# Windowed attention with sink keys: 64-row score matmuls on the two halves of the array, two head pairs at a time

## The chip, the cores and the metric

The kernel runs on one core of a Trainium2 chip. The metric is the device time of one execution in microseconds. The core has five engines that run their own instruction streams and wait for each other by semaphores: PE (TensorE, matmuls, with weight loads shown apart as PEld), DVE (VectorE), ACT (ScalarE), POOL (GpSimd) and SP, which here issues the DMA transfers.

## The reference

Three stages follow one another, for 2 sequences of 768 positions.

```python
# 1. attention: 8 heads of 64, each query sees 128 keys back and the first 4 (the sinks)
scores = 1/sqrt(64) * q @ k.T
keep   = (pos_k < n_sink) | ((pos_q - pos_k >= 0) & (pos_q - pos_k < window))   # n_sink 4, window 128
a      = softmax(where(keep, scores, -1e9));  x = a @ v
# 2. MLP, 512 -> 1024 -> 512
h = relu(x @ w_in);  y = (h * sigmoid(conv3(h))) @ w_out
# 3. second attention, 4 experts of width 64, causal, top 2 by a gate
out = sum over chosen e of gate_e * softmax(causal(q_e @ k_e.T / 8)) @ v_e @ wo_e
```

The weights of the MLP come as float64 words and are turned into pairs of float32r numbers (a high and a low part) on the chip.

## The kernel before

Sequences are called b0 and b1. Attention goes over query tiles of 128 positions (`qt`, 6 for each sequence) and, inside a tile, over 4 pairs of heads (`pr`): 24 steps for each sequence. One step is `a1_S` (scores on PE, masked minimum on DVE at L427, exponent on ACT at L430), `a1_T` (PE transposes at L532, copied out by ACT at L494) and `a1_V` (products with the values, L574). Once for each query tile come the row sums' inverse (L489, L490), its transpose (L501) and broadcast through DRAM, the sink keys' part (L554 to L582), the scaling of the output (L516) and its split into high and low parts (L494, L604).

A score tile is [128 queries, up to 260 keys] for one head. A head has only 64 features, and the two heads of a pair lie in partitions 0 to 63 and 64 to 127. The kernel before multiplies with all 128 rows: the query tile of one head is padded with zeros in the other head's 64 rows, so the keys of both heads can stream through. The padded tiles are two buffers of [128, 4 pairs, 2 heads, 128], cleared once at the start (L1151, L1152), and one query tile is loaded by two transfers of 64 partitions (L258). In b0 a head's scores are one matmul of up to 260 columns (L425), in b1 two of 130 (L413), since there each key tile has its own buffer. These are float32 matmuls, and the trace shows two weight loads and two matmul records for each. The value products write 64 output columns for each head (weights 128x64), the two heads of a pair to the two halves of the output partitions.

The order of the work is a table. A phase has stages with a lag in slots; `run_phases` puts step i of a stage into slot `start + floor(lag + i * rate)`, and inside a slot the order of the names in `ORD1` (attention and MLP) or `ORD2` (second attention) decides. Engines work through their streams in that order. The conversion of the MLP weights (L291 to L303 on DVE, L351 on POOL) is cut into pieces that `background` strews over the slots. b1's attention runs in the same slots as the MLP of b0 (L742, L745 to L771, L786). The second attention has scores (L996, L997), transposes (L1034), value products (`a2_V`, L1053, again 128x64 weights) and the output matmul (`a2_W`, L1077), for each query tile in two steps, one for each pair of experts. All PE results go through 8 PSUM buffers called psB.

Of the kernel before, what the change touches and what calls it, by code (L numbers as in the profile page):

```python
# [70 lines left out]
SPLIT_LOAD = (5, 2)  # L71
SPLIT_FROM = (NT, NT)
SPLIT_LO = (1, 1)
LAGS = ((1, 2, 1, 4, 3, 4, 5, 5, 2, 7, 7, 9, 11), (1, 1, 2, 3, 4, 5, 6, 3, 2, 6, 7, 8, 8))
# [3 lines left out]
ORD1 = 's0.hi m.rest a0.more a1.T s1.lo a0.gather m.more m.H a1.gather a1.rB m.gate a0.xl m.Y a1.S a1.sV a1.xl a1.r a0.S a1.halo a0.sL late a0.V a0.rB a0.sV a0.xm a1.more s0.lo a1.sT a0.halo a0.rT s1.hi a1.xm a1.misc a1.V a1.xh a0.sT a0.T a0.misc a1.sL a0.r a1.rT m.conv s1.load s0.load m.misc a0.xh'  # L78
ORD2 = 'q1 c0.V c0.T c0.S0 c1.norm c1.V c1.T c1.S0 out c0.W c0.S1 qlo c0.norm c1.W in c1.S1 q0'
SPLIT_LO_ENG = ('pp', 'pp')  # L80
# [4 lines left out]
ENG_KQ = ('da', 'aa')  # L85
# [4 lines left out]
ATTN_LOADS = ((3, 'q', 0, 2), (3, 'v', 0, 3), (7, 'q', 0, 3), (17, 'v', 0, 4), (11, 'q', 0, 4), (19, 'v', 0, 5), (16, 'q', 0, 5), (21, 'v', 1, 0), (20, 'v', 1, 1), (33, 'v', 1, 2), (35, 'v', 1, 3), (40, 'v', 1, 4), (47, 'v', 1, 5), (19, 'k', 1, 0), (19, 'q', 1, 0), (23, 'k', 1, 1), (24, 'q', 1, 1), (25, 'k', 1, 2), (27, 'q', 1, 2), (30, 'k', 1, 3), (33, 'q', 1, 3), (34, 'k', 1, 4), (37, 'q', 1, 4), (38, 'k', 1, 5), (42, 'q', 1, 5))  # L90
class Kernel:
    def __init__(self, tc, q, k, qd, kd, v, vs, lim, w_in, conv_w, w_out, wqkv, wo, out):
        self.tc, self.nc = tc, tc.nc
        self.q, self.k, self.qd, self.kd, self.v, self.vs, self.lim = q, k, qd, kd, v, vs, lim
# [54 lines left out]
    def consts(self, pool):  # L149
# [10 lines left out]
        self.mEO = [pool.tile([P, 2, KW], F32, name=f"m{i}x") for i in range(3)]  # L160
# [22 lines left out]
    def masks(self):  # L183
# [16 lines left out]
        def rest():  # L200
# [11 lines left out]
            for t in range(2):  # L212
                nc.gpsimd.tensor_copy(self.mEO[2][:, t], self.mEO[0][:, 1 - t])
# [23 lines left out]
    def load_qkv(self, b, n, lo, hi):  # L237
# [7 lines left out]
        if n == "k":  # L245
            hi = min(hi, SPLIT_FROM[b])
            if hi <= lo:
                return
# [136 lines left out]
    def a1_S(self, b, qt, pr):  # L385
# [12 lines left out]
        else:  # L398
            m = self.mEO[2 if self.ring(b, qt) and qt % 2 == 0 else qt % 2]
            N, mask = 2 * KW, m.rearrange("p t c -> p (t c)")  # L400
        split = self.ring(b, qt)
        for j in range(2) if split else ():
            h, me = 2 * pr + j, slice(j * D, (j + 1) * D)
            ts_, cs = slice(0, min(qt + 1, 2)), slice(0 if qt > 1 else 2, KW)
            dst = ps[j][:, :N].rearrange("p (t c) -> p t c", t=ts_.stop)
            nc.tensor.matmul(dst, self.QS[:, h, :], self.KH[:, ts_, h, cs], start=True, stop=False)
            nc.tensor.matmul(dst, self.QS[me, h, :], self.KL[me, ts_, pr, cs], start=False, stop=True)
        for j in range(0 if split else 2):
            if b:
                w = N // min(qt + 1, 2)  # L410
                for c in range(N // w):
                    rhs = t["k", max(qt - 1, 0) + c][:, pr, KW - w :]
                    nc.tensor.matmul(ps[j][:, c * w : (c + 1) * w], t["q", qt][:, pr, j, :], rhs, start=(c == 0),  # L413
                                     stop=(c == N // w - 1), skip_group_check=True)
                continue
            if qt == 0:
                rhs = t["k"][:, 0, pr, 2:]
                dst = ps[j][:, :N]
            elif qt == 1:
                rhs = t["k"][:, 0:2, pr, 2:]  # L420
                dst = ps[j][:, :N].rearrange("p (t c) -> p t c", t=2)
            else:
                rhs = t["k"][:, qt - 1 : qt + 1, pr, :]
                dst = ps[j][:, :N].rearrange("p (t c) -> p t c", t=2)
            nc.tensor.matmul(dst, t["q", qt][:, pr, j, :], rhs, start=True, stop=True)  # L425
# [8 lines left out]

    def ring(self, b, qt):

        return qt >= SPLIT_FROM[b]

    def split_load(self, b, qt, n, hf):

        w = KW if n == "k" else P
        raw = self.wraw[n, b, qt, hf] = self.Wt([P, 4, w], s="raw" + n)
        src = (self.kd if n == "k" else self.qd)[b, :, qt, 4 * hf : 4 * hf + 4, :]
        for r in range(2):
            self.nc.sync.dma_start(raw[r * D : (r + 1) * D], src)

    def split(self, b, qt, n, hf):


        nc = self.nc  # L450
        if not hasattr(self, "QS"):
            self.QS = self.Rt([P, H, P], s="QS")
            ring = self.Kt([P, 2 * H * KW + 2 * NPAIR * KW], F32R, "ring")
            self.KH = ring[:, : 2 * H * KW].rearrange("p (s h c) -> p s h c", s=2, h=H)
            self.KL = ring[:, 2 * H * KW :].rearrange("p (s a c) -> p s a c", s=2, a=NPAIR)
        raw = self.wraw.pop((n, b, qt, hf))
        hs = slice(4 * hf, 4 * hf + 4)
        hi = self.KH[:, qt % 2, hs, :] if n == "k" else self.QS[:, hs, :]
        self.copy(ENG_KQ[b]["kq".index(n)], hi, raw)
        self.wraw["lo", n, b, qt, hf] = raw, hi  # L460

    def split_lo(self, b, qt, n, hf):
        raw, hi = self.wraw.pop(("lo", n, b, qt, hf))
        pr = slice(2 * hf, 2 * hf + 2)
        eng = self.nc.gpsimd if SPLIT_LO_ENG[b]["kq".index(n)] == "p" else self.nc.vector
        for j in range(2):
            rows = slice(j * D, (j + 1) * D) if n == "k" else slice((1 - j) * D, (2 - j) * D)
            r, h = (x.rearrange("p (a j) c -> p a j c", j=2)[rows, :, j, :] for x in (raw, hi))
            lo = self.KL[rows, qt % 2, pr, :] if n == "k" else h
            eng.tensor_tensor(lo, r, h.bitcast(F32), op=ALU.subtract)  # L470

    def split_phase(self, b):

# [5 lines left out]
        def each(fn):  # L479
            return lambda i: fn(*steps[i]) if self.ring(b, steps[i][1]) or steps[i][2] == "k" else None  # L480
# [793 lines left out]
```

## Time and profile before

| | |
|---|---|
| median of 3 runs | 388.13 us (387.78 to 388.64) |
| profiled execution | 388.33 us, of it 386.5 us from the first to the last instruction (the span) |
| PE busy | 97% of the span |
| weight loads busy | 88% |
| DVE busy | 75% |
| ACT, POOL busy | 66%, 38% |
| attention alone / with the MLP of b0 / MLP of b1 / projections and second attention | about 0 to 60 / 60 to 160 / 160 to 245 / 245 to 386 us |

Busy shares are means over stages with different limits, so the prediction reads them by stretches. A matmul's printed duration holds its way through the array; how many follow each other in a given time is read from the chain of waits, which lists the pieces of work that released one another, or from the starts in the timeline. Each record is one pass. A few per cent of the matmul records can be missing.

### The profile page before, as it was taken

Reading aid. Unit: us, or ns where it says so; the run is one execution under the profiler, and the core shown is the slowest. Engines: PE = TensorE matmul, PEld = TensorE weight load, DVE = VectorE, ACT = ScalarE, POOL = GpSimd, SP = SyncE. Lnnn points to the kernel's source line nnn. Section 1 sums busy time; section 2 is a strip of 40 time slices with the busy share of each in tenths; the row PEclk is TensorE's granted clock in tenths of the full one; section 3 lists DMA queues with packets and bytes.
Section 4 is the critical chain, followed back from the end, with each engine's and each line's share of the span. In section 5 each row is a group of like instructions: output and inputs, shape, how many; then the busy total and the mean of one; then the engine's idle time right before and its main releaser. Section 6 shows DMA issues by size and latency. Waiting matters only on the chain.

```text
span 386.5 us, 8883 instructions
## 1 busy us (share of the span) xinstructions
PE 375.2 (97%) x3161; PEld 340.3 (88%) x3161; DVE 289.0 (75%) x849; ACT 256.2 (66%) x743; POOL 146.8 (38%) x248
## 2 busy tenths in 40 slices
PE   7899999979999999999999999999999999999994
PEld 5577778969998999999999999999999899888873
DVE  5689999999999798768865767237779786666711
ACT  4887886654676546545665875439888888778741
POOL 8226323465556264575521322310034325134400
PEclk9999999989999999999999999999999999999999
DMA  6944658333253301010221010000000000010112
GB/s 184 319 132 136 194 171 231 121 111 115 78 164 111 111 2 39 18 30 2 50 55 43 20 43 13 3 2 0 2 2 1 3 27 29 31 56 28 56 48 72
DMA packets 22660, 27.53 MB, mean 71 GB/s; under 512 B 2160, under 2 KB 15824, under 8 KB 22608
## 3 DMA queue, kind: packets, MB, share of 16 engines
q1 hardware_dynamic: 22608, 26.88, 23.0%
q8 instruction: 27, 0.44, 0.5%
q14 instruction: 25, 0.20, 0.2%
HBM read 23.68 MB, written 3.19 MB: 70 GB/s over the span
## 4 chain that ended last, share of the span: by engine, by line
PE 83%; DVE 10%; DMA 3%; issue 2%; ACT 1%; SPq 0%; ACTq 0%; DVEq 0%
PE psB L786 18%; PE psB L742 17%; PE psB L934 9%; PE psB L1053 6%; PE psB L1034 6%; PE psB L1077 5%; PE psB L862 4%; PE psB L413 3%; PE psB L574 3%; PE psB L532 3%; DMA q<-in_q_dram 3%; DVE P L427 3%; PE psB L997 3%; PE psB L996 3%; PE psB L425 2%
## 5 line engine op out<-in xcount | busy, mean ns | idle before, releaser
L786 PE MATMUL psB<-g,wouthf 128*128 128x256 f32 x384 | 70.1, 281 | 0.0
L430 ACT ACTIVATE P<-P,nm 128x260 f32<-128x260 f32 (+2 forms) x96 | 46.6, 487 | 22.4 <-DVE nm L427 22.1
L1022 POOL TENSOR_SCALAR P<-P,r 128x256 f32<-128x256 f32 (+5 forms) x48 | 30.1, 640 | 80.7 <-ACT v L874 29.6
L786 PEld LDWEIGHTS psB<-g,wouthf 128*128 128x128 f32 x384 | 59.2, 189 | 0.0
L742 PE MATMUL psB<-xh,winhf 128*128 128x258 f32 x192 | 57.3, 298 | 1.4 <-ACT PT L494 1.2
L742 PE MATMUL psB<-xh,winlf 128*128 128x258 f32 x192 | 54.9, 286 | 0.0
L742 PE MATMUL psB<-xl,winhf 128*128 128x258 f32 x192 | 54.7, 285 | 0.0
L771 POOL TENSOR_TENSOR g<-ht,g 128x256 fp32r<-128x256 f32 x48 | 34.1, 711 | 53.7 <-ACT g L765 49.6
L786 PE MATMUL psB<-g,woutlf 128*128 128x256 f32 x192 | 54.0, 281 | 0.0
L758 ACT ACTIVATE ht<-ht 128x256 f32<-128x256 f32 x48 | 20.1, 418 | 33.4 <-DVE ht L756 33.3
L742 PEld LDWEIGHTS psB<-xh,winhf 128*128 128x128 f32 x192 | 36.9, 192 | 2.2 <-ACT PT L494 1.4
L763 DVE SCALAR_TENSOR_TENSOR ht<-ht 128x256 f32<-128x256 f32 x48 | 23.6, 491 | 19.0 <-ACT ht L758 19.0
L742 PEld LDWEIGHTS psB<-xl,winhf 128*128 128x128 f32 x192 | 37.1, 193 | 0.0
L742 PEld LDWEIGHTS psB<-xh,winlf 128*128 128x128 f32 x192 | 36.9, 192 | 0.0
L786 PEld LDWEIGHTS psB<-g,woutlf 128*128 128x128 f32 x192 | 36.3, 189 | 0.0
L765 ACT CAST g<-ht 128x256 fp32r<-128x256 f32 x48 | 19.1, 398 | 18.5 <-DVE ht L763 17.4
L1007 ACT ACTIVATE P<-P,nm 128x256 f32<-128x256 f32 (+3 forms) x48 | 26.7, 558 | 6.2 <-DVE nm L1001 5.7
L756 DVE SCALAR_TENSOR_TENSOR ht<-ht,cw 128x256 f32<-128x256 f32 x48 | 28.8, 601 | 1.7
L532 PE MATMUL psB<-ident,P 128*128 128x128 f32 x176 | 29.7, 286 | 0.1
L574 PE MATMUL psB<-PT,v 128*64 128x128 f32 x352 | 29.7, 286 | 0.0
L749 POOL TENSOR_SCALAR ht<-ht,cw 128x256 f32<-128x256 f32 x24 | 16.6, 690 | 32.1 <-ACT ht L745 27.2
L1001 DVE CUSTOM_DVE_ANT_0 P<-psB,causal 128x256 f32<-128x256 f32 (+3 forms) x48 | 22.6, 487 | 6.8 <-PE psB L997 6.5
(168 smaller groups left out, 1043.0 us busy)
## 6 DMA issues: line engine op xcount, KB each, us to landing
raw<-in_w_in_dram SPq DMA_DIRECT2D x8, 512.0 KB, 3.4
raw<-in_w_out_dram SPq DMA_DIRECT2D x8, 512.0 KB, 3.7
q<-in_q_dram SPq DMA_DIRECT2D x24, 128.0 KB, 4.4
v<-in_v_dram SPq DMA_DIRECT2D x12, 256.0 KB, 3.6
R<-rD SPq DMA_DIRECT2D x24, 128.0 KB, 3.1
out_dram<-ot SPq DMA_DIRECT2D x11, 256.0 KB, 2.0
k<-in_k_dram SPq DMA_DIRECT2D x8, 260.0 KB, 4.0
raw<-in_wqkv_dram SPq DMA_DIRECT2D x8, 193.0 KB, 2.5
```

What stands on the lines that cost most here:

```text
L430: nc.scalar.activation(Pt[:, j, :N], Pt[:, j, :N], AF.Exp, bias=nmx[:, j : j + 1], scale=-1.0, accum_out=sums[:, j : j + 1])
L532: nc.tensor.transpose(ps[:, j, c, :], Pt[:, j, c0 : c0 + P], self.ident)
L574: nc.tensor.matmul(o[j * D : (j + 1) * D, pr, :], t["v", kt][:, h * D : (h + 1) * D], PT[:, j, c, :], start=(pr == 0 and c == 0), stop=(qt ...
L742: nc.tensor.matmul(ps[:, :XW], w[:, f, kc, :], x[:, kc, :], start=(i == 0), stop=(i == len(ops) - 1))
L756: nc.vector.scalar_tensor_tensor(t1, h[:, 2 : 2 + CH], self.cw[:, 2 * NF + f : 2 * NF + f + 1], t1, op0=ALU.mult, op1=ALU.add)
L763: nc.vector.scalar_tensor_tensor(t1, t1, 1.0, h[:, 1 : 1 + CH], op0=ALU.add, op1=ALU.mult)
L771: eng.tensor_tensor(g[:, 1], t1, g[:, 0].bitcast(F32), op=ALU.subtract)
L786: nc.tensor.matmul(self.m1y[d // 2][:, d % 2, :], w[:, f, d, :], g[:, k], start=(first and i == 0 and d % 2 == 0), stop=(last and i == 2), ...
L934: nc.tensor.matmul(ps, w[:, kc, c0 : c0 + P], y[:, kc, :], start=(i == 0), stop=(i == len(ops) - 1))
L1007: nc.scalar.activation(Pt[:, lo:hi], src, AF.Exp, bias=nm[:, 0:1], scale=sg, accum_out=sums[:, j, i : i + 1])
L1022: nc.gpsimd.tensor_scalar(Ps[j][:, :N], Ps[j][:, :N], r[:, j : j + 1], 1.0, op0=ALU.mult, op1=ALU.mult)
L1034: nc.tensor.transpose(ps[:, s, :], Ps[j][:, c * P : (c + 1) * P], self.ident)
```

## The change

The query buffers hold no zeros any more: there are four of [128, 4 pairs, 128] in the same memory, and a query tile is one transfer of 128 partitions with 2 KB for each partition in one piece. A score matmul takes 64 rows of queries and 64 rows of keys, and goes over one key tile (up to 130 columns) in both sequences. The two heads of a pair alternate, so that neighbouring matmuls use the upper and the lower rows of the array. A stage can have a group size g: step i is then put where the first step of its group stands. Scores and value products of the first attention, and value products and output matmul of the second, have g = 2. The lag of b1's value products goes from 3 to 4 slots, the names in `ORD1` stand in another order (a1.V and a0.V right behind a1.S and a0.S), and one value tile of b1 is loaded 3 slots earlier. Code for a split of the scores that no step used (`ring`, `split_*`), and a third mask with its two copies on POOL, are gone.

```diff
-        for m, (lag, fn) in enumerate(stages):
+        for m, (lag, fn, *g) in enumerate(stages):
             for i in range(n):
-                at.setdefault(o + math.floor(lag + i * rate), []).append((k, m, i, fn))
+                first = i - i % g[0] if g else i
+                at.setdefault(o + math.floor(lag + first * rate), []).append((k, m, i, fn))
...
-LAGS = ((1, 2, 1, 4, 3, 4, 5, 5, 2, 7, 7, 9, 11), (1, 1, 2, 3, 4, 5, 6, 3, 2, 6, 7, 8, 8))
+LAGS = ((1, 2, 1, 4, 3, 4, 5, 5, 2, 7, 7, 9, 11), (1, 1, 2, 4, 4, 5, 6, 3, 2, 6, 7, 8, 8))
...
-                t[n, tt] = self.qbuf[tt % 2]
-                for j in range(2):
-                    rows = slice(j * D, (j + 1) * D)
-                    self.nc.sync.dma_start(t[n, tt][rows, :, j, :], src[rows, tt].rearrange("p (a c) -> p a c", c=P))
+                t[n, tt] = self.qbuf[(b * NT + tt) % len(self.qbuf)]
+                self.nc.sync.dma_start(t[n, tt], src[:, tt].rearrange("p (a c) -> p a c", c=P))
...
+        w = N // min(qt + 1, 2)
+        for c in range(N // w):
+            for j in range(2):
+                rows = slice(j * D, (j + 1) * D)
+                kt = t["k", max(qt - 1, 0) + c] if b else t["k"][:, max(qt - 1, 0) + c]
+                nc.tensor.matmul(ps[j][:, c * w : (c + 1) * w], t["q", qt][rows, pr, :], kt[rows, pr, KW - w :],
+                                 start=(c == 0), stop=(c == N // w - 1), skip_group_check=True)
...
-            "xm": (xm, last(self.x_norm)), "S": (0, each(self.a1_S)), "T": (tr, each(self.a1_T)),
-            "V": (pv, each(self.a1_V)), "gather": (gather, each(self.a1_gather)), "sT": (sT, last(self.a1_sinkT, 2)),
+            "xm": (xm, last(self.x_norm)), "S": (0, each(self.a1_S), 2), "T": (tr, each(self.a1_T)),
+            "V": (pv, each(self.a1_V), 2), "gather": (gather, each(self.a1_gather)), "sT": (sT, last(self.a1_sinkT, 2)),
...
-              "V": (A2_V, each(self.a2_V)), "W": (A2_V + 1, each(self.a2_W))}
+              "V": (A2_V, each(self.a2_V), 2), "W": (A2_V + 1, each(self.a2_W), 2)}
...
-                self.qbuf = [self.Rt([P, NPAIR, 2, P], F32, "q") for _ in range(2)]
+                self.qbuf = [q[:, i] for q in (self.Rt([P, 2, NPAIR, P], F32, "q") for _ in range(2)) for i in range(2)]
```

How the order moves is shown at three places. The first is PE in the middle of b0's attention, before: two steps. L425 are scores (one row a head), L574 value products (two heads in each row), L532 four transposes; the names are PSUM buffer, then the operands.

```order
L425 MATMUL psB_404<-k_124,q_117 128x260
L425 MATMUL psB_405<-k_124,q_117 128x260
L574 MATMUL psB_351<-PT_335,v_131 64x128 x2
L574 MATMUL psB_351<-PT_335,v_133 64x128 x2
L532 MATMUL psB_419<-ident,P_373 128x128 x4
L425 MATMUL psB_434<-k_124,q_117 128x260
L425 MATMUL psB_435<-k_124,q_117 128x260
L574 MATMUL psB_351<-PT_364,v_131 64x128 x2
L574 MATMUL psB_351<-PT_364,v_133 64x128 x2
L532 MATMUL psB_448<-ident,P_406 128x128 x4
```

The same place after the change (scores are L397 there, value products L495, transposes L453); two more score rows of the first pair of heads stand ahead of these.

```order
L397 MATMUL psB_405<-k_119,q_117 128x130
L397 MATMUL psB_406<-k_119,q_117 128x130
L397 MATMUL psB_417<-k_119,q_117 128x130
L397 MATMUL psB_418<-k_119,q_117 128x130
L397 MATMUL psB_417<-k_119,q_117 128x130
L397 MATMUL psB_418<-k_119,q_117 128x130
L495 MATMUL psB_362<-PT_333,v_124 64x128 x2
L495 MATMUL psB_362<-PT_333,v_126 64x128 x2
L495 MATMUL psB_362<-PT_379,v_124 64x128 x2
L495 MATMUL psB_362<-PT_379,v_126 64x128 x2
L453 MATMUL psB_438<-ident,P_352 128x128 x4
L453 MATMUL psB_453<-ident,P_407 128x128 x4
```

Scores of two steps, value products of two steps and transposes of two steps now stand together, and the scores run straight into the value products.

The second place is PE near the end of the second attention, before: value products of the last two query tiles (L1053) and the output matmul (L1077) of the tile ahead of each; zh and zl are the two parts of the attention's result.

```order
L1053 MATMUL psB_5469<-PT_1062_5355,v_710_3968 64x128 x4
L1077 MATMUL psB_5474<-wohf,zh_5446 128x512 x2
L1077 MATMUL psB_5474<-wolf,zh_5446 128x512 x2
L1077 MATMUL psB_5474<-wohf,zl_5447 128x512 x2
L1053 MATMUL psB_5469<-PT_1069_5393,v_710_3968 64x128 x4
L1053 MATMUL psB_5492<-PT_1072_5410,v_710_3968 64x128 x4
L1053 MATMUL psB_5492<-PT_1074_5417,v_723_4034 64x128 x4
L1053 MATMUL psB_5492<-PT_1076_5424,v_736_4098 64x128 x2
```

After the change (value products L972, output matmul L996):

```order
L972 MATMUL psB_5500<-PT_1066_5401,v_710_3989 64x128 x4
L972 MATMUL psB_5500<-PT_1069_5415,v_710_3989 64x128 x4
L996 MATMUL psB_5513<-wohf,zh_5509 128x512 x2
L996 MATMUL psB_5513<-wolf,zh_5509 128x512 x2
L996 MATMUL psB_5513<-wohf,zl_5510 128x512 x2
L972 MATMUL psB_5523<-PT_1076_5452,v_710_3989 64x128 x4
L972 MATMUL psB_5523<-PT_1078_5459,v_723_4055 64x128 x4
L972 MATMUL psB_5523<-PT_1080_5466,v_736_4119 64x128 x2
```

Both value products of the last tile but one (psB_5500) are now neighbours, and the output matmul that reads their result (zh_5509) is the very next instruction; before, the first products of the last tile stood between.

The third place is SP at the start, before: transfers in the order in which they are issued (k, q and v tiles of b0, the raw weights, the row sums rD).

```order
L251 DMA k_124<-in_k_dram 128x1040
L258 DMA q_117<-in_q_dram 64x4x128 x2
L261 DMA v_238<-in_v_dram 128x512
L505 DMA rD_284<-rT_282 8x128
L265 DMA vs_315<-in_vs_dram 128x512
L258 DMA q_118<-in_q_dram 64x4x128 x2
```

After the change:

```order
L243 DMA k_119<-in_k_dram 128x1040
L248 DMA q_117<-in_q_dram 128x512
L251 DMA v_228<-in_v_dram 128x512
L426 DMA rD_278<-rT_276 8x128
L255 DMA vs_325<-in_vs_dram 128x512
L248 DMA q_117<-in_q_dram 128x512
```

The order is the same; each query tile is one transfer, and the third and fourth tile go to the second buffer (two slots of q_117) and no longer overwrite tiles that are still read.

## Rows read from the trace of the kernel before

**Rows 1.** The page's chain that ended last: share of the span by engine

```profile
PE 83%; DVE 10%; DMA 3%; issue 2%; ACT 1%; SPq 0%; ACTq 0%; DVEq 0%
```

**Rows 2.** Stretches: length, busy PE, PEld, DVE, ACT, POOL, then clock, DMA share, GB/s

```profile
24.00:53.00 29.00, 28.77 (x229) 21.14 (x230) 28.40 (x89) 24.82 (x79) 13.34 (x29) 1.00 0.57 170
53.00:98.00 45.00, 42.83 (x373) 38.09 (x370) 43.93 (x118) 27.41 (x90) 22.05 (x35) 0.96 0.50 146
98.00:120.00 22.00, 22.00 (x199) 20.78 (x198) 21.52 (x51) 14.44 (x43) 11.70 (x20) 1.00 0.33 104
120.00:160.00 40.00, 39.78 (x356) 37.54 (x355) 35.23 (x90) 24.76 (x74) 19.45 (x37) 1.00 0.20 60
```

**Rows 3.** Chain of waits around 28 us, b0: start us, us, what

```profile
27.50 0.60 DVE xl L604
28.10 0.34 DVE P L427
...
28.80 0.60 DVE f64u L303
```

**Rows 4.** Chain of waits, then timeline of DVE, at the third query tile

```profile
9.95 8.72 DMA q<-in_q_dram
...
19.52 0.43 DVE L427 CUSTOM_DVE_ANT_0 P<-psB,m0x 128x260 f32<-128x260 f32 x1 [1.78 <-PE psB L425]
```

**Rows 5.** Chain of waits, a step of b0 and scores of a b1 step

```profile
43.01 0.88 PE psB L425 x4
43.89 0.59 PE psB L574 x8
44.47 0.59 PE psB L532 x4
...
123.72 0.89 PE psB L413 x8
```

**Rows 6.** Groups by form: weight loads of scores and value products; last numbers busy, mean ns

```profile
L413 PEld LDWEIGHTS psB<-k,q 128*128 128x128 f32 x176 | 21.6, 191 | 0.0
L574 PEld LDWEIGHTS psB<-PT,v 128*64 128x64 f32 x352 | 18.2, 136 | 10.1 <-issue 5.4 <-ACT xh L494 0.7 <-DVE xl L604 0.3
```

**Rows 7.** Timeline of PEld, value products at 41.65 us: start us, us, what

```profile
41.65 0.14 PEld L574 LDWEIGHTS psB<-PT,v 128*64 128x64 f32 x2 [0.34 <-issue]
```

**Rows 8.** Chain of waits in the second attention

```profile
290.82 1.09 PE psB L1034 x10
...
354.74 0.37 PE psB L1053 x4
...
366.76 1.02 PE psB L1053 x16
367.79 1.24 PE psB L1034 x10
...
376.57 1.59 PE psB L1077 x6
```

**Rows 9.** Instructions of L413 alone in a stretch: length, busy PE, PEld

```profile
120.00:160.00 40.00, 7.39 (x56) 6.84 (x56) 1.00 0.20 60
```

**Rows 10.** Group of the copy that the output matmul waits for

```profile
L132 ACT CAST zh<-psB 128x256 fp32r<-128x256 f32 x11 | 4.0, 366 | 1.6 <-PE psB L1053 1.4
```

**Rows 11.** Timeline of SP at the start: start us, us, what

```profile
1.64 1.37 SPq L258 DMA_DIRECT2D q<-in_q_dram  x2
...
3.70 1.26 SPq L258 DMA_DIRECT2D q<-in_q_dram  x2
5.00 1.08 SPq L261 DMA_DIRECT2D v<-in_v_dram  x2
```

**Rows 12.** A stretch at the start, columns as in rows 2

```profile
12.00:18.00 6.00, 5.59 (x38) 3.69 (x36) 4.58 (x21) 5.32 (x21) 0.00 (x0) 1.00 1.06 338
```

**Rows 13.** A stretch at the lower clock (columns as in rows 2)

```profile
80.00:82.00 2.00, 0.79 (x4) 0.78 (x4) 1.97 (x5) 1.18 (x3) 1.08 (x2) 0.79 0.06 20
82.00:84.00 2.00, 2.00 (x12) 2.00 (x11) 2.00 (x8) 1.51 (x5) 2.00 (x4) 0.50 0.87 280
```

**Rows 14.** Chain of waits: the same MLP matmuls at the lower and the full clock

```profile
81.23 2.95 PE psB L742 x12
...
86.99 1.43 PE psB L742 x12
```

More of the change, by code (lines that the diff above doesn't have):

```diff
@@ L77 @@
 EVT = 'aaadadada'
-ORD1 = 's0.hi m.rest a0.more a1.T s1.lo a0.gather m.more m.H a1.gather a1.rB m.gate a0.xl m.Y a1.S a1.sV a1.xl a1.r a0.S a1.halo a0.sL late a0.V a0.rB a0.sV a0.xm a1.more s0.lo a1.sT a0.halo a0.rT s1.hi a1.xm a1.misc a1.V a1.xh a0.sT a0.T a0.misc a1.sL a0.r a1.rT m.conv s1.load s0.load m.misc a0.xh'
+ORD1 = 'm.rest a0.more a1.T a0.gather m.more m.H a1.gather a1.rB m.gate a0.xl m.Y a1.S a1.V a1.sV a1.xl a1.r a0.S a0.V a1.halo a0.sL late a0.rB a0.sV a0.xm a1.more a1.sT a0.halo a0.rT a1.xm a1.misc a1.xh a0.sT a0.T a0.misc a1.sL a0.r a1.rT m.conv m.misc a0.xh'
 ORD2 = 'q1 c0.V c0.T c0.S0 c1.norm c1.V c1.T c1.S0 out c0.W c0.S1 qlo c0.norm c1.W in c1.S1 q0'
-SPLIT_LO_ENG = ('pp', 'pp')
 ENG_G = 'pp'
@@ L159, in consts @@
         self.m1 = pool.tile([P, 2 * P], F32, name="m1")
-        self.mEO = [pool.tile([P, 2, KW], F32, name=f"m{i}x") for i in range(3)]
+        self.mEO = [pool.tile([P, 2, KW], F32, name=f"m{i}x") for i in range(2)]
     def limits(self):
@@ L211, in rest @@
                 pen(e, m[:, 1, 0:2], snk[:, 2 - first : 4 - first])
-            for t in range(2):
-                nc.gpsimd.tensor_copy(self.mEO[2][:, t], self.mEO[0][:, 1 - t])
         self.more_masks = rest
@@ L398, in a1_S @@
         else:
-            m = self.mEO[2 if self.ring(b, qt) and qt % 2 == 0 else qt % 2]
+            m = self.mEO[qt % 2]
             N, mask = 2 * KW, m.rearrange("p t c -> p (t c)")
[L401 to L425, printed above, removed]
+        w = N // min(qt + 1, 2)
[5 more added lines that the diff above has]
+                                 start=(c == 0), stop=(c == N // w - 1), skip_group_check=True)
         for j in range(2):
@@ L433, in a1_S @@
         self.a1Pg[(b, qt, pr)] = Pt
[L435 to L472, printed above, removed]
-        f = max(SPLIT_FROM[b] - 1, 0)
-        steps = [(b, qt, n, hf) for qt in range(f, NT) for hf in range(2) for n in "kq"]
-        rate = RATE1 if b else 1
-        at = (4 * f - 3) * rate
-        def each(fn):
-            return lambda i: fn(*steps[i]) if self.ring(b, steps[i][1]) or steps[i][2] == "k" else None
-        st = {"load": (at - SPLIT_LOAD[b], each(self.split_load)), "hi": (at, each(self.split)),
-              "lo": (at + SPLIT_LO[b], each(self.split_lo))}
-        n = len(steps) if SPLIT_FROM[b] < NT else 0
-        return lambda names: (b * NSTEP, n, [st[n] for n in names.split()], rate)
     def a1_r(self, b, qt):
@@ L526, in a1_T @@
         else:
-            cols = [KW + 2, 2] if self.ring(b, qt) and qt % 2 == 0 else [2, KW + 2]
+            cols = [2, KW + 2]
         nb = len(cols)
@@ L650, in go0 @@
                 if i == at:
[L651 to L652 removed]
+                    self.load_qkv(bb, n, lo, lo + 1)
             if i >= 4:
@@ L1198, in program @@
                 a0, a1 = first
-                src = {"a0": a0, "a1": a1, "m": m, "s0": self.split_phase(0), "s1": self.split_phase(1), "late": late}
+                src = {"a0": a0, "a1": a1, "m": m, "late": late}
                 ph = self.order(ORD1, src)
@@ L1210 @@
     lim = lim.bitcast(I32)[None, :].to_broadcast([P, 4])
-    K = Kernel(tc, q, k, qd, kd, v, vs, lim, w_in, conv_w, w_out, wqkv, wo, out)
+    K = Kernel(tc, q, k, v, vs, lim, w_in, conv_w, w_out, wqkv, wo, out)
     with tc.tile_pool(name="const", bufs=1) as cpool:
```

23 lines of the change are left out of this document (5 added, 18 removed).

## The prediction

> **What bounds the kernel now.** I read the chain that ended last first: 83% of the span is PE, 10% DVE, 3% a transfer [rows 1]. That is a mean, so next the stretches [rows 2]. From 24 to 120 us DVE has 93.85 of 96 us busy, and the chain runs through it, item behind item, softmax next to weight conversion [rows 3]; PE looks as busy there, but where DVE fills its time a shorter matmul only makes PE wait. From 120 to 160 us PE is full and DVE idles 4.77 us: here a shorter matmul counts until DVE is full too. From 160 us on nearly all of the chain is PE, with no attention score of the changed kind in it; the second attention at its end is changed in its value products. At the start the chain holds one transfer, 8.72 us from the issue of the third query tile to its landing [rows 4], and DVE idles 1.78 us behind it.
>
> So the reader has to keep two sums: what PE is spared, and how much of it DVE lets through.
>
> **The scores on PE.** A step of b0 takes 0.88 us for four records of 260 columns, a step of b1 0.89 us for eight of 130 [rows 5], so 0.22 and 0.111 us a record; PE streams them one behind the other. After the change every step has eight records of 130 columns and 64 rows (half as many of 128 columns in each sequence's first tile). Nothing in this trace uses half the rows. The nearest thing uses half the columns: the value products. There two weight loads with a mean of 136 ns [rows 6] are done within 0.14 us [rows 7], so both halves load at once, and 4 records take 0.37 us, 16 take 1.02 [rows 8]: (1.02 - 0.37) / 12 = 0.054 us a record, and 0.37 - 4 x 0.054 = 0.15 fixed. One record alone needs about 0.11, as the scores of b1 show, so two run side by side.
>
> For the new scores the ends are these. If halves of rows work as halves of columns do, two steps (16 records) cost 1.02 us, the 0.15 included. If they don't, they cost 16 x 0.111 + 0.15 = 1.93, slightly more than now (1.77). I take 1.02: it is the row that also packs two matmuls into the array.
>
> The Trainium skill has a rule against this: by its page "TensorE: Matmul & The Clock Gate", section "LDWEIGHTS (loading the stationary operand)", a weight load takes its time by columns, and one of 32 rows takes as long as one of 128. No load here has fewer than 128 rows, so no row shows it. By it each score load stays at the 191 ns of [rows 6], hidden behind matmuls of the other half only if both halves may load at once; if not, the sum is that of the first rival below. The Trainium skill says on the same page, section "Part 3: Packing small matmuls", that loads overlap running matmuls of another row group, which speaks for 1.02.
>
> **Changing between shapes.** Transposes right behind value products take 1.24 us for ten, elsewhere 1.09 [rows 8]: 0.15 us on leaving the half-array shape, and about 0.15 on entering it (the fixed part above). Before, a step has two such changes, a pair of steps four. After, a pair has three: full to scores, scores to value products, back to full. The Trainium skill, "TensorEngine Tiling (Array Packing)", section "Key Properties", says that a change of the tiling mode drains the array; the trace agrees with its 0.15 us. Counted by it the scores, which used to be free of this, now pay too, and that is in the sum here.
>
> **A pair of steps on PE.** Before: 2 x (0.88 + 0.59 + 0.59) = 4.12 us for scores, value products and transposes [rows 5]. After: 1.02 + 1.02 + 0.15 + 8 x 0.109 = 3.06 (0.109 being a tenth of 1.09). Spared: 1.06 us a pair, 0.53 a step. Over 20 pairs, and some 0.6 in each of the 4 shorter ones, PE is spared 23 us. If all of that counted, the kernel would gain 6%; it won't.
>
> **What counts of it.**
>
> 24 to 120 us: DVE's work is not changed (two clears at the start are gone, before the first scores), and its idle time is 0.60 + 1.07 + 0.48 = 2.15 us [rows 2]. No more than that can be won, and nothing is the other end. I take 1.1. What is late next here is DVE itself.
>
> 120 to 160 us: 56 records of L413 [rows 9] are 7 steps, 7 x 0.53 = 3.7 us spared on PE; DVE has 4.77 us to spare. The two don't wait at the same moments, and four score buffers are now asked for at once instead of two. Ends 0.5 and 3.7, I take 2.8.
>
> Second attention: in the PE order 23 groups of value products become 12. Each one less saves 0.15 + 0.15: 11 x 0.30 = 3.3 us, and PE is the chain there [rows 8]. Against it stands one new wait. The output matmul of the last tile but one now stands directly behind its value products, and needs ACT's copy of them, 0.37 us [rows 10]; before, value products of the last tile covered that (the 1.59 us in [rows 8] for its six records hold no such wait). Behind it on PE stand the last 20 value products, so the end waits. Price 0.37 to 0.73 (the copy twice over, for the hand-overs). Net 2.6 to 2.9; I take 2.6.
>
> Start: a query tile took two issues, 1.37 and 1.26 us for the first two tiles; one transfer of the same size and shape as v's takes 1.08 / 2 = 0.54 [rows 11]. So the third tile's issue comes up to 1.55 us earlier (1.37 + 1.26 - 2 x 0.54), and no longer waits for the first tile's scores to be read. But the transfers are full then: share 1.06, 338 GB/s [rows 12], and the bytes ahead of it are the same. They can only gain by starting earlier. Ends 0 and the 1.78 us that DVE idles [rows 4]; I take 1.0. The first scores themselves wait for the mask, which the change leaves alone.
>
> At nothing I put the third mask's two copies on POOL (POOL is idle for 6 us behind them [rows 12]), the value tile loaded 3 slots earlier, and b1's value products one slot later: they have PE's order to themselves and only hold a PSUM buffer longer, which is in the 120 to 160 us range.
>
> Sum: 1.1 + 2.8 + 2.6 + 1.0 = 7.5 us. The profiled execution took 388.3 us, 0.2 above the median of 388.13; so 380.8 for it and **380.6 us** for the median.
>
> **Rivals.**
>
> *A: the halves of rows don't load or run side by side.* The change then doesn't do what it says. For it: every score record keeps a full-width load of 191 ns, longer than the 136 ns that the column halves show. Against it: the column halves do both at once. PE is spared 4.12 - 3.97 = 0.15 us a pair. Then 24 to 120 gives 0.2, 120 to 160 0.5, the second attention 2.6 and the start 1.0: 388.1 - 4.3 = 383.8 us.
>
> *B: DVE is no wall.* If DVE's idle time closes fully, 2.15 + 3.7 + 3.3 + 1.8 = 11 us: 377.1. For it: PE is as full as DVE from 24 to 120 us [rows 2], so DVE's waits there can be waits for PE. Against: two engines that hand work to each other seldom lose all their waits.
>
> *C: slower, by the clock.* At 81 us PE, after a stretch in which it was busy 0.79 of 2 us, was granted 0.50 of its clock (1.2 GHz instead of 2.4) for some 3 us [rows 13], and 12 matmuls took 2.95 instead of 1.43 [rows 14]. With the change PE has less work where DVE sets the pace. Per pair it needs about 3.6 us (3.06 and 0.5 for sinks, sums and the rest) against DVE's 4.2 (28.4 us for some 13.4 steps), so it waits in every pair. A pair at the lower clock takes PE 7.2 us, 3.0 more than DVE's pace. Three such pairs eat the 7.5 us; with five of the ten between 30 and 80 us it is 388.1 - 7.5 + 15 = 395.6 us. Against it: the fall stood alone; from 12 to 18 us PE also waited (5.59 of 6 us busy) and kept 1.00 [rows 12].
>
> **Chances.** Forecast 0.64, its own range 377.5 to 383 (its terms from 5 to 10.5 us). A 0.12, B 0.12, C 0.07. The remaining 0.05 is no difference, within 0.2% (0.8 us, about what a measurement here can tell): the gain of the second attention spent on waits for PSUM buffers. Faster by more than that: 0.64 + 0.12 + 0.12 = 0.88, less 0.02 for a bad end of A, 0.86; same 0.06; slower 0.08. The range from 376 to 386 takes in B and A and leaves out C.
>
> **What would show it.** The score line's records start in couples a few ns apart, its share of the chain in b1 falls from 0.89 us a step to about 0.5; if records follow each other at 0.11 us, A holds. DVE's busy time between 24 us and the end of b1's scores stays as it is, its idle time shrinks, and PE gets waits there that end on DVE or ACT. The chain in the second attention has 12 groups of L1053's successor. The third query tile lands about a microsecond earlier. The granted clock below 1.00 for more than 10 us in all would mean C. The forecast is wrong if the attention's part, from the start to the last score of b1, is shorter by more than 8 us or by less than 2.

## The result and the profile after

The changed kernel takes 391.25 us (median of 8 runs, 389.62 to 392.61) against 387.97 for the kernel before on the same chip: a ratio of 1.007, 95% interval 1.0047 to 1.0094 (one median divided by the other gives 1.0085). The forecast was 380.6 us; the change made the kernel about 0.7% slower. The profiled execution took 389.77 us, its span is 387.9. That is 1.5 us below the median, so the profiles before and after lie 1.4 us apart where the medians lie 3.3 apart.

The page's chain that ended last, by engine, answers to [rows 1]:

```profile
PE 68%; DVE 20%; ACT 5%; issue 4%; DMA 1%; POOL 0%; DVEq 0%; ACTq 0%
```

PE has lost 15 points of the chain, DVE has won 10. The stretches of [rows 2] (length, then busy PE, PEld, DVE, ACT, POOL, clock, DMA share, GB/s) are now:

```profile
24.00:53.00 29.00, 22.86 (x263) 18.94 (x258) 25.07 (x83) 23.49 (x76) 12.70 (x29) 0.94 0.52 156
53.00:98.00 45.00, 40.39 (x385) 35.75 (x383) 43.17 (x118) 27.55 (x91) 21.28 (x33) 0.96 0.43 136
98.00:120.00 22.00, 19.19 (x162) 18.06 (x162) 20.22 (x47) 13.70 (x40) 11.15 (x21) 0.92 0.38 122
120.00:160.00 40.00, 36.36 (x355) 34.06 (x355) 34.67 (x89) 23.36 (x71) 21.72 (x36) 1.00 0.19 60
```

From 24 to 160 us PE idles 17.2 us where it idled 2.6. The spared matmul time shows as idle time. But DVE, which should have stayed full, idles more as well: 12.9 us instead of 6.9. Both engines wait, and the clock falls in three of the four stretches.

The matmuls do what was forecast. The chain of waits around 30 us (start us, us, what):

```profile
30.05 0.27 PE psB L422
30.32 0.48 PE psB L453 x4
30.81 1.09 PE psB L397 x16
31.90 1.02 PE psB L495 x16
32.93 0.26 PE psB L475
33.19 0.87 PE psB L453 x8
```

Scores of two steps (L397) take 1.09 us, value products of two steps (L495) 1.02, eight transposes 0.87. That is 2.98 for a pair, 3.06 was forecast. One score load, by the groups by form, is not shorter than the 191 ns of [rows 6] (its mean takes in the stretches at the lower clock). The second line is from the timeline of the weight loads:

```profile
L397 PEld LDWEIGHTS psB<-k,q 64*128 64x128 f32 x352 | 24.4, 203 | 7.0 <-issue 2.3 <-DMA k<-in_k_dram 1.7 <-ACT PT L415 1.4
...
30.74 0.64 PEld L397 LDWEIGHTS psB<-k,q 64*128 64x128 f32 x10 [0.17 <-issue]
```

Ten loads are done within 0.64 us. One every 0.111 us, as the full-row records of [rows 5] come, they would need 9 x 0.111 + 0.19 = 1.19 us. So the two halves of rows load and run side by side. The Trainium skill says on its page "TensorE: Matmul & The Clock Gate", section "LDWEIGHTS (loading the stationary operand)", that a load's time goes by its columns and not by its rows; the trace agrees with 203 ns for 64 rows against 191 for 128. On the same page, section "Part 3: Packing small matmuls", it says that loads overlap running matmuls of another row group; the trace agrees with 16 records, loads included, in 1.09 us.

What is new is a wait. PE's waits from 24 to 160 us (us in total, times, longest), first the only one at the sums' transpose before, then those after:

```profile
PE psB L501 <- DVE su L490: 1.0, 2, 0.8
```

```profile
PE psB L422 <- DVE su L411: 7.9, 4, 2.6
PE psB L422 <- ACT P L403: 2.6, 2, 1.7
PE psB L495 <- ACT y L718: 1.8, 1, 1.8
PE psB L422 <- DVE nm L400: 1.8, 1, 1.8
```

L422 is the transpose of the row sums' inverse (L501 before). PE waits 12.3 us in front of it here, in seven waits. One of these waits, in the timelines of DVE and of PE (start us, us, engine, line; idle time before it in brackets):

```profile
38.36 0.42 DVE L400 CUSTOM_DVE_ANT_0 P<-psB,m0x 128x260 f32<-128x260 f32 x1
38.70 0.08 DVE L400 DVE_READ_ACCUMULATOR2_ANT nm<- 128x1 f32 x1
38.70 0.69 DVE L293 SCALAR_TENSOR_TENSOR f64u<-raw,f64u 128x512 int32<-128x512 int32 x1
39.31 0.17 DVE L410 TENSOR_SCALAR su<-su 128x8 f32<-128x8 f32 x1
39.51 0.20 DVE L411 RECIPROCAL su<-su 128x8 f32<-128x8 f32 x1
```

```profile
39.86 0.27 PE L422 MATMUL psB<-ident,su 128*8 128x128 f32 x1 [2.63 <-DVE su L411]
```

DVE first reads four score tiles of the next pair (37.31 to 38.78 us), then a piece of the weight conversion, and only then inverts the sums for which PE is standing. The next pair's scores stand behind the transpose on PE. So each such wait of PE keeps back the scores that DVE needs next. DVE's own idle time is spread over many waits; the costliest from 24 to 160 us is for scores, 4.6 us in four waits against 3.4 in five before:

```profile
DVE P L400 <- PE psB L397: 4.6, 4, 1.9
```

Behind some of these waits the clock falls. Two stretches, columns as above:

```profile
48.78:52.20 3.42, 3.42 (x25) 2.86 (x26) 1.51 (x7) 2.21 (x7) 1.03 (x1) 0.50 0.72 226
103.40:106.80 3.40, 3.40 (x18) 3.40 (x17) 3.29 (x10) 3.13 (x12) 0.17 (x1) 0.50 0.02 5
```

There are four such stretches at 1.2 GHz, 17 us in all (the others from 7.8 and 65.9 us); before, once the clock had risen, there was one up to the last matmuls, in [rows 13]. Sixteen score records take 2.09 us at 49.90.

Where the time went, by the same event in both traces (after minus before, us; attention exponents and MLP tanhs counted from the start): the 17th exponent -0.5, the 29th -1.5, the 45th +0.6, the 65th +1.6, the 93rd +3.4. These are each the first of a pair of steps. A pair's exponents stand together after the change, so the last of the same pairs come out lower: the 20th -1.7, the 32nd -3.1, the 48th -0.9, the 68th -2.4, the 96th, which is the last, -0.1. Free of this are the tanhs: the first +0.3, the last of b0 +2.3, all of b1's +2.3 to +2.4; then the first exponent of the second attention +2.3 and the end of the span +1.4. So up to the MLP's first tanh (75 us) the changed kernel is level with the one before, and it falls behind where b1's pairs run among the MLP's instructions.

### The profile page after: what moved, and what is told of

Its sections match the earlier page's. It is cut to its first block, busy times and chain, and to the rows that moved or that the text cites. A ratio compares the mean times of both kernels' runs of the same rounds, so it can differ in the third digit from the quotient of the medians.

```text
span 387.9 us, 8998 instructions
## 1 busy us (share of the span) xinstructions
PE 359.8 (93%) x3241; PEld 332.0 (86%) x3241; DVE 283.9 (73%) x847; ACT 255.0 (66%) x743; POOL 147.7 (38%) x244
## 4 chain that ended last, share of the span: by engine, by line
PE 68%; DVE 20%; ACT 5%; issue 4%; DMA 1%; POOL 0%; DVEq 0%; ACTq 0%
PE psB L705 14%; PE psB L661 14%; PE psB L853 8%; PE psB L972 5%; PE psB L953 5%; PE psB L781 4%; PE psB L996 4%; DVE P L400 4%; PE psB L453 3%; PE psB L397 3%; PE psB L916 2%; PE psB L915 2%; PE psB L495 2%; DVE ht L674 2%; DVE f64u L293 2%
## 5 line engine op out<-in xcount | busy, mean ns | idle before, releaser
L453 PE MATMUL psB<-ident,P 128*128 128x128 f32 x176 | 29.9, 293 | 3.1 <-DVE nm L400 1.6
L397 PE MATMUL psB<-k,q 64*128 64x130 f32 (+1 forms) x352 | 29.5, 305 | 2.5 <-ACT PT L415 1.2
L397 PEld LDWEIGHTS psB<-k,q 64*128 64x128 f32 x352 | 24.4, 203 | 7.0 <-issue 2.3
L668 POOL TENSOR_SCALAR ht<-ht,cw 128x256 f32<-128x256 f32 x24 | 17.7, 736 | 30.8 <-ACT ht L664 29.1
```

The costliest lines, as they stand in the source:

```text
L397: nc.tensor.matmul(ps[j][:, c * w : (c + 1) * w], t["q", qt][rows, pr, :], kt[rows, pr, KW - w :], start=(c == 0), stop=(c == N // w - 1), ...
L453: nc.tensor.transpose(ps[:, j, c, :], Pt[:, j, c0 : c0 + P], self.ident)
```

## The experiments

All were timed in five rounds beside the kernel before, which took 388.1 to 388.4 us in them. Profiles of kernels with the same code up to the second attention differ by up to 0.9 us, from the third query tile's transfer on, so what I read from profiles below is read inside a stretch, and the times are medians.

### 1. The sums ahead

```diff
-ORD1 = '... m.Y a1.S a1.V a1.sV a1.xl a1.r a0.S a0.V ... a1.sL a0.r a1.rT ...'
+ORD1 = '... m.Y a0.r a1.r a1.S a1.V a1.sV a1.xl a0.S a0.V ... a1.sL a1.rT ...'
```

> The changed kernel with one edit: the row sums' inverse (stages a0.r and a1.r) stands ahead of the scores of its slot instead of behind them. Theory S (sums): in the changed kernel PE waits 13 us in all at the transpose of the row sums, because DVE reaches the inverse only behind the four score reads of the next pair. Then these waits shrink below 5 us, the clock falls with them to fewer than two times 3.4 us, and the time comes to 383 to 386 us (from 391.3). Theory P (pairs): any group of two pairs makes PE and DVE work in turns, whatever stands first; then the waits move to the transposes of P or to the scores, and the time stays at 389 to 392. Theory K (clock): PE has too little work where DVE sets the pace, the clock falls anyway, 389 to 392 with 10 us or more at half clock.

388.51 us, ratio 1.0008 (0.9988 to 1.0027), 2.7 below the changed kernel. PE's waits from 24 to 160 us:

```profile
PE psB L422 <- DVE nm L400: 3.4, 2, 1.8
PE psB L453 <- ACT P L403: 2.9, 5, 0.7
```

The wait in front of the sums' transpose went from 12.3 to 3.4, as theory S had it, but the time fits none of the three: PE's idle time went only from 17.2 to 14.2 us, since waits at the transposes behind it (L453) took its place. Up to 67 us this kernel runs 2.2 to 3.4 us ahead of the kernel before, by the first exponent of each pair, and its first tanh is 3.2 early; then, among the MLP's matmuls, it loses the lead (b0's last tanh is 1.2 late).

### 2. No pairs in the first attention

```diff
-"S": (0, each(self.a1_S), 2)
-"V": (pv, each(self.a1_V), 2)
+"S": (0, each(self.a1_S))
+"V": (pv, each(self.a1_V))
```

> The changed kernel without the groups of two in the first attention's scores and value products (second attention unchanged, order of names and lags as in the change). Theory P: the turns go, DVE is again full from 24 to 120 us, 383 to 386 us. Theory S: the inverse then stands behind two score reads instead of four, so about half of the 13 us of waits at the row sums goes, 386 to 389. Theory K: the clock falls as often as in the changed kernel, 389 to 392.

388.67 us, 1.001 (0.9994 to 1.0027), in theory S's range. The pairs, too, are needed for the loss; taking them out gives no gain over before, though the scores still use half the rows each.

### 3. The 64-row scores alone

The kernel before with the `a1_S` and the query buffers of the change, its own order, no groups.

> The kernel before with the 64-row scores and the unpadded queries alone: no groups, old order of names, old lags. By the prediction's sums PE is spared 0.4 us a step less two shape changes a step, and DVE lets 3 to 4 us of it through: 384 to 385.5 us. Theories S and P: no loss here, 384 to 386, since nothing stands behind a group. Theory K: the clock falls three or more times, 388 to 392.

388.72 us, 1.0005 (0.9989 to 1.0022), not 384 to 386; theory K had the time, but without falls of the clock its reason is out. The whole stretch from 24 to 160 us:

```profile
24.00:160.00 136.00, 127.27 (x1201) 107.02 (x1198) 129.41 (x345) 91.06 (x283) 67.09 (x119) 1.00 0.37 116
```

The sums of [rows 2] are 133.4 for PE and 129.1 for DVE. PE is spared 6.1 us, there are no new falls of the clock, and none of it counts. In 120 to 160 us, where the forecast wanted 2.8 us, DVE waited for scores 2.8 us before and waits 2.5 now. The first row is of the kernel before, the second of this one:

```profile
DVE P L427 <- PE psB L413: 2.8, 3, 1.2
```

```profile
DVE P L407 <- PE psB L404: 2.5, 3, 1.3
```

It is three single waits, each for scores that stand in PE's order behind MLP matmuls (24 of them, some 2.9 us, ahead of the longest).

### 4. The second attention's groups alone

```diff
-"V": (A2_V, each(self.a2_V)), "W": (A2_V + 1, each(self.a2_W))
+"V": (A2_V, each(self.a2_V), 2), "W": (A2_V + 1, each(self.a2_W), 2)
```

> The kernel before with the groups of two in the second attention alone. By the prediction 2.6 us less, 385.4 us. If the second attention of the changed kernel is any guide (it took 0.9 us less than before from the first projection to the end), 387.1: the spared shape changes are then eaten by waits for the softmax, and the trace shows them ahead of the output matmul and the transposes.

387.22 us, 0.9977 (0.9962 to 0.9991): 0.9 us, not 2.6. I added up, for each line, by how much its matmuls' ends advance PE's time from 273 us on: value products 21.80 before and 20.73 here, transposes 21.34 and 19.84, output matmuls 17.41 and 19.12. So 2.6 us were won (2.9 without a new gap of 0.37 ahead of value products), and 1.7 given back. The chain of waits around the last tile but one:

```profile
372.60 0.38 ACT zh L133
372.98 0.04 issue
373.03 1.65 PE psB L1078 x6
```

There are such waits at four of the twelve output matmuls, not only at this one, and the other three are not for ACT's copy but for zl, the low part, which DVE makes. PE's waits behind 300 us:

```profile
PE psB L1078 <- ACT zh L133: 0.5, 1, 0.5
PE psB L1078 <- DVE zl L134: 0.4, 2, 0.3
PE psB L1054 <- ACT zh L133: 0.4, 1, 0.4
```

The third of those for zl, at 302 us, is 0.09 us long and not in the list. The matmuls of zl advance PE by 1.3 us more than before, those of zh by 0.4.

### 5 and 6. DVE's work lowered, with and without 64-row scores

Both leave out two of the five passes of the weight conversion; 5 is the kernel before, 6 the kernel of experiment 3.

```diff
-            nc.vector.scalar_tensor_tensor(st["u"], w1, -0x40000000, st["u"], op0=ALU.bitwise_and, op1=ALU.bitwise_or)
...
-            nc.vector.scalar_tensor_tensor(st["u"], w0, 29, st["u"], op0=ALU.logical_shift_right, op1=ALU.bitwise_or)
```

> The kernel before with two of DVE's five passes in each weight conversion left out (the sign and the low word, 16 conversions, so the weights are magnitudes cut to 20 bits): 12.0 + 10.9 = 22.9 us less work on DVE, everything else as before. It is the ground for the run with the 64-row scores. Theory W (DVE's work is the wall of the attention, and PE stands just behind it): PE idles only 2.6 of the 136 us from 24 to 160 in the kernel before, so no more than some 2.5 to 3.5 us come free; 385 us. Theory T (the engines wait for each other in turns, so it isn't the amount of DVE's work): below 1.5 us; 387 us.

> The same two passes left out of the kernel before with 64-row scores and unpadded queries (no groups, old order), whose PE idled 8.7 of the 136 us from 24 to 160 and which took 388.7 with all passes. Theory W: with DVE's wall lowered by 22.9 us the spared PE time comes through: 380 to 382, 4 to 6 below the run without it. Theory T: the two stay within 1.5 us of each other, 386 to 387.

383.14 us (0.9856, 0.983 to 0.9883) and 378.27 (0.972, 0.9693 to 0.9748): 4.9 us between them. Each alone is 2 to 3 us lower than I expected, the difference is as theory W had it. DVE's costliest wait from 24 to 160 us, in 5 and in 6:

```profile
DVE ht L762 <- ACT ht L757: 4.0, 7, 0.8
```

```profile
DVE P L406 <- PE psB L403: 10.6, 15, 1.9
```

The same edit is worth nothing (388.72) with DVE's full work and 4.9 us with 22.9 us less of it. DVE's work is the wall that keeps the shorter scores from counting.

### 7. Sums ahead, pairs in the first sequence only

```diff
-"S": (0, each(self.a1_S), 2)
-"V": (pv, each(self.a1_V), 2)
+"S": (0, each(self.a1_S), 2 - b)
+"V": (pv, each(self.a1_V), 2 - b)
```

> The changed kernel with the row sums' inverse ahead of the scores, and with pairs in the first sequence only (the second sequence's steps one by one; second attention as changed). Theory: the loss of the sums-ahead kernel after 67 us comes from the bursts of pairs among the MLP's instructions, so without them most of its lead of 2.3 to 3.4 us is kept, the granted clock does not fall after 100 us, and the second attention adds 1: 385 to 386. Rival: the lead is lost at the MLP's start whatever the pairs do, because DVE's work is the wall there: 387.5 to 388.5.

383.59 us, 0.9865 (0.9839 to 0.9891), better than I expected. The lead stays: 3.2 us at the 53rd exponent, 3.4 at the 93rd. The granted clock stays at 1.00 from 12.8 to 381 us in the profiled execution.

### 8. The output matmul a slot later

```diff
-"W": (A2_V + 1, each(self.a2_W), 2)
+"W": (A2_V + 1, each(self.a2_W))
```

on the kernel of experiment 4; a tile's output matmul now comes two slots behind its value products.

> The kernel before with the second attention's value products in groups, but the output matmul one slot later, where other value products stand between. The groups alone took 387.2: values and transposes 2.9 us shorter, output matmuls 1.7 longer (waits of 0.35 to 0.7 us for the copies of the values at four of the twelve, behind 300 us). Theory: three of these four waits go, 1.0 to 1.5 us: 385.7 to 386.2. Rival: they only move, since the value and output buffers are held longer and the scores wait for them: 387.2 within 0.3.

385.56 us, 0.993 (0.9906 to 0.9953). Output matmuls advance PE by 17.2 us, as before the groups, and the gain of 2.6 to 2.9 that was forecast for this part is there: 2.85 (388.41 - 385.56).

### 9. Both together

Experiment 7 with the edit of experiment 8.

> The kernel with pairs in the first sequence only and the sums ahead (383.59 us), with the second attention's output matmul one slot later as well (worth 387.22 - 385.56 = 1.66 us where it was tried alone). The two lie in stretches that have nothing in common, so they should add: 381.9, within 0.5. If the second attention's gain depended on what went before, 383 to 384.

381.90 us, 0.984 (0.9819 to 0.9861): as expected, and the shortest of the kernels here with all of the computation, 6.5 us below the kernel before.

### 10 and 11. Which of the two edits makes the lead

10 is the changed kernel with the diff of experiment 7 alone (sums late), 11 that of experiment 1 with the diff of experiment 2 (sums ahead, no pairs).

> The changed kernel with one edit: the second sequence's first attention goes step by step, its pairs are taken out (sums late as in the change, pairs in the first sequence). Theory: the loss has two parts, the late sums in the first sequence (at the first tanh of the MLP the changed kernel stands 2.9 us behind the one with sums ahead) and the pairs among the MLP's instructions (sums-ahead kernel 388.51 with them, 383.59 without): so 383.6 + 2.9 = 386.5, 386 to 387. Rival: with late sums the pairs of the first sequence are a loss by themselves and the rest is the same: 388.5 or more.

> The changed kernel with the sums ahead and no pairs in the first attention at all (second attention as changed). Theory: the lead of 3 us comes from pairs and sums together, since without pairs the sums stand right behind the scores whose exponentials they need and DVE waits inside them (0.40 us an instruction against 0.20): 387.5 to 388.7, as the kernel without pairs and with late sums (388.67). Rival: the place of the sums alone makes the lead: 384 to 385.

388.36 us (0.9995, 0.998 to 1.0011) and 387.77 (0.998, 0.9966 to 0.9994). The first missed: not 386 to 387, but close to the rival's 388.5. The second lies in its theory's range, but not for its reason: the first of the two instructions for the sums takes 0.16 to 0.38 us in it, and nothing like a wait inside it is seen. All have the second attention's groups; medians in us:

| | no pairs | pairs in b0 | pairs in both |
|---|---|---|---|
| sums late | 388.67 | 388.36 | 391.25 |
| sums ahead | 387.77 | 383.59 | 388.51 |

Pairs in b0 gain 4.2 us with the sums ahead and nothing with the sums late. Pairs in b1 lose 4.9 and 2.9.

### 12 to 14. The clock's share

Ten matmuls of zeros ahead of the row sums' transpose; in 12 in both sequences, in 13 in the first only, in 14 as in 13 but on the kernel of experiment 10.

```diff
-        ps = self.psB()[:H, :P]
+        box = self.psB()
+        for _ in range(0 if b else 10):
+            self.nc.tensor.matmul(box[:, 256:512], self.zeros[:, :P], self.zeros, start=True, stop=True)
+        ps = box[:H, :P]
```

> The changed kernel with ten matmuls of zeros (256 columns, about 1.07 us together at full clock) ahead of each transpose of the row sums, where PE idles 13.0 us in all in front of L422, and where each of the four falls of the granted clock (17 us in all at 0.50) begins. They need only a free PSUM buffer, so they run in the wait. Theory: the falls go and the clock's part of the loss with them, 389.0 to 390.3. Rival: the falls go and the time does not (391.2 within 0.6), because DVE's row sums set the pace there and PE at half clock still gets its work done in time. If the falls stay, matmuls of zeros do not count for the clock.

> The changed kernel with the ten matmuls of zeros ahead of the row sums' transposes of the first sequence only. With them in both sequences no fall of the granted clock was left between the start and 100 us, and the first tanh of the MLP came 1.6 us earlier than in the changed kernel; the loss came after it, among the MLP's matmuls. Theory: the falls in the first sequence cost the change some 1.6 us: 389.2 to 390.2. Rival: what was won by 75 us is lost again in the second sequence, where the fall at 103 us and the pairs stay: 391.2 within 0.5.

> The kernel with late sums and pairs in the first sequence only (388.36 us; its clock falls at 7, 31, 41 and 82 us) with the same matmuls of zeros ahead of the first sequence's row sums' transposes. Its exponentials lose 1.6 us against the kernel before between the 28th and the 36th, and 1.3 between the 36th and the 44th, the two places where its clock is at 0.50. Theory: late sums cost by the clock that falls behind them, so most of those 2.9 us comes back: 386 to 387. Rival: they cost by DVE's and PE's turns alone: 388.4 within 0.5.

12 took 392.62 us (1.0125, 1.0104 to 1.0147), above its theory and its rival: b0's falls were gone and the MLP's first tanh came 1.6 us earlier, but among the MLP's matmuls the added ones cost more. 13 took 390.03 (1.005, 1.0029 to 1.0071), 14 took 387.33 (0.9971, 0.996 to 0.9982): 1.2 and 1.0 us below the kernels that they fill. The same two stretches in experiment 10 and, behind it, in 14 (columns as above):

```profile
31.20:34.50 3.30, 3.30 (x30) 2.74 (x27) 2.87 (x11) 2.23 (x9) 0.48 (x3) 0.50 0.31 115
41.40:44.80 3.40, 3.40 (x30) 3.10 (x30) 3.14 (x10) 2.14 (x8) 1.50 (x3) 0.50 0.84 263
```

```profile
31.20:34.50 3.30, 3.30 (x45) 2.84 (x45) 3.09 (x11) 2.51 (x10) 0.88 (x3) 1.00 0.38 131
41.40:44.80 3.40, 3.40 (x49) 2.94 (x47) 3.08 (x12) 2.38 (x10) 1.07 (x4) 1.00 0.93 294
```

So filling b0's waits gains 1.0 to 1.2 us, within what 13's theory had, and between 14's theory (1.4 to 2.4) and its rival (within 0.5). The 1.2 us alone is not clear of the noise, since the intervals of the changed kernel and of 13 overlap. Nor does it bound what the clock costs in all: four of 13's twelve executions had a mean clock of 0.993 or more and took 388.4 to 388.9 us, the others had 0.985 or less and took 389.0 to 392.1. In 14's profile the clock is at 1.00 from 12.8 to 81 us, and late sums still cost 3.7 us (387.33 against 383.59; its fastest execution, 386.64, is 2.5 above the slowest of 7). PE's costliest wait there:

```profile
PE psB L425 <- DVE su L411: 4.2, 5, 1.5
```

## Why the prediction was wrong

**The sign.** The likeliest case, faster by 7.5 us, failed. Two edits of the change decide it. With the sums left late, the pairs of b0 gain nothing (388.67 without them, 388.36 with them), and the pairs of b1 lose 2.9 us (391.25 with them, 388.36 without), which is most of what makes the changed kernel slower than the one before. Rival C, the slower one, had the right sign, and by its sign (more than 10 us below a clock of 1.00) it holds: 17 us. Its price does not: it put 3.0 us on each pair at the lower clock, and the three stretches that the fill of b0 removes, 13.7 us at 0.50, are worth 1.0 to 1.2 us together. What the clock is worth in the second sequence (the fall at 103 us) was not tried by itself.

**The pair on PE: right.** 2.98 us against 3.06, the halves side by side (rival A is out). What PE is spared is real; the 6.1 us of experiment 3 show it.

**24 to 120 us, 1.1: the step that failed first.** I bounded this term by 2.15 and nothing, on the ground that DVE's work does not change. Its work did not, its order did. With a pair, DVE has four score tiles to read ahead of the row sums instead of two, and the scores of the next pair stand behind the sums' transpose on PE. That wait is in no term of the sum: I had moved the scores in my account and not asked what they are moved past on DVE. Experiments 1, 7, 10 and 14 show it: with the place of the sums as the only edit 391.25 becomes 388.51, and 388.36 becomes 383.59.

**120 to 160 us, 2.8: wrong.** Here I read DVE's 4.77 us of idle time as room that a shorter score would use. Experiment 3 spares PE 6.1 us from 24 to 160 and gains nothing. The idle time is a few single waits behind MLP matmuls, which stay as long. A stretch in which PE is full and DVE is not is not yet one in which each microsecond of PE counts: what matters is which PE work DVE waits for. And pairs in b1, whose steps run from about 54 to 159 us, cost 2.9 to 4.9 us, the opposite sign; that it is the burst of a pair among the MLP's instructions is argued from where the lead is lost, not shown apart from PSUM buffers and clock.

**Second attention, 2.6: the saving right, the waits mis-sized.** Groups save 2.9 us there (3.3 forecast). I priced one wait, for ACT's copy, at 0.37 to 0.73; the output matmuls give back 1.7 us in four waits, three of them for the low part from DVE, which is in no term of the sum. Without them (experiment 8) the part gains 2.85.

**Start, 1.0: half of it.** DVE's wait at the third tile went from the 1.78 us of [rows 4] to 0.40. But the mask on which the first scores wait is itself later: the limits are read at 4.03 us instead of 3.54, although their transfer is issued first in both kernels (3.8 to 4.1 in the kernels with one transfer for a query tile, 3.5 in those with two). And the first of the four falls of the clock lies here, so the stretch of [rows 12] is now at 0.78 (last line). Before, then after:

```profile
3.54 0.17 DVE L166 CAST wf<-words 128x4 f32<-128x4 int32 x1 [1.39 <-DMA words<-in_lim_dram]
```

```profile
4.03 0.17 DVE L163 CAST wf<-words 128x4 f32<-128x4 int32 x1 [3.04 <-DMA words<-in_lim_dram]
...
19.04 0.43 DVE L400 CUSTOM_DVE_ANT_0 P<-psB,m0x 128x260 f32<-128x260 f32 x1 [0.40 <-PE psB L397]
...
12.00:18.00 6.00, 5.88 (x57) 4.33 (x53) 4.83 (x25) 4.55 (x16) 0.00 (x0) 0.78 0.67 249
```

By the 17th exponent 0.5 us was left.

**Rival B, no wall: out.** DVE's work is the wall (experiments 3, 5 and 6). By the stated sign (the attention, up to the last score of b1, shorter by under 2 us) the forecast was to be called wrong, and it is: that score starts at 157.0 us instead of 157.8, and b0's MLP beside it has its last tanh 2.3 us later.

What stays open is why pairs and sums ahead gain 4.2 us together when DVE has the same instructions. The profiles of experiments 11 and 7 end 3.3 us apart, and 2.4 of these are there at the 17th exponent (21.1 and 18.7 us), where the chain of waits still runs through PE and not DVE. The first 24 us, in 11 and behind it in 7:

```profile
0.00:24.00 24.00, 21.10 (x153) 14.41 (x155) 13.94 (x67) 14.70 (x52) 8.64 (x21) 1.00 0.68 234
```

```profile
0.00:24.00 24.00, 20.95 (x183) 15.97 (x183) 16.43 (x76) 16.66 (x60) 10.66 (x25) 1.00 0.75 253
```

DVE gets 2.5 us more of its work done there. Two things differ: the pairs have fewer changes of shape, and the granted clock rises earlier. It is recorded from its rise to 1.00 on, 16.1 us in 11 and 12.8 in 7, so the column does not show it, but the scores do: eight take 1.16 us at 13.4 us and 0.65 at 16.3 in 11, sixteen take 2.01 at 10.9 and 1.09 at 14.4 in 7. The two were not taken apart. The records of the conversion on DVE (L281 to L293) sum to 56.2 us in 11 and 53.6 in 7, but to 53.1 in 10, which gains nothing; so shorter passes are not the reason by themselves.

## What to carry to other kernels

Where two engines hand work to each other, a matmul that is made shorter counts only where the other engine waits for that matmul; take the other engine's work away in an experiment and see whether the gain appears, before tuning on. Work done in groups moves every small result that is due at a group's end, such as a row sum: put it ahead of the next group's work on its engine, and put a consumer a slot behind its producer when the grouping has taken away what covered the copy. Use groups only in the stretch where they pay: here the first sequence and the second attention, 381.9 us, and not among the MLP.

## What was not expected of the hardware

A pass of the weight conversion on DVE usually takes 0.42 or 0.69 us, by its kind; some take about 1.0 us longer. In experiment 11 there are twelve long ones, and each starts 0.1 to 0.4 us behind the start of a POOL pass and ends 0.3 to 0.6 us behind its end. One of them on DVE, and its neighbour on POOL, from their timelines:

```profile
29.28 1.63 DVE L293 SCALAR_TENSOR_TENSOR f64u<-raw,f64u 128x512 int32<-128x512 int32 x1
```

```profile
29.10 1.27 POOL L266 TENSOR_TENSOR vsr<-vs,vsr 32x512 fp32r<-32x512 f32 x1 [2.42 <-issue]
```

DVE's pass ends 0.54 us after POOL's, about as if it had begun only when POOL was done. The Trainium skill says so on its page "SBUF — State Buffer", section "Terms": DVE and GpSimd lock a shared port pair for a whole instruction, and the loser blocks. The trace agrees with these 1.63 us against 0.69. So a part of what the profile calls busy on DVE is waiting, and the wall depends on when POOL works; no experiment here moves this alone.

Matmuls of zeros ahead of a waiting instruction kept the granted clock at 1.00 in stretches that had been at 0.50 (the two shown for experiments 10 and 14). They pay only where PE has nothing else to do: 1.0 to 1.2 us won in the first sequence, 2.6 lost where they also stand among the MLP's matmuls (392.62 against 390.03).
